# Moving one row tile's load and statistics, and the place of the shift rows, in the start of a fused adaLN block

## The chip, the cores and the metric

The kernel runs on one core of a Trainium2 chip. The metric is device time in microseconds (us) of one launch; the times shown are medians over several launches. A profile belongs to one launch: its "span" reaches from the first instruction of the program to the last, and the launch's own time is a little longer than that.

The engines that matter are TensorE (PE; its weight loads have rows of their own, PEld), VectorE (DVE), ScalarE (ACT), GpSimd (POOL) and the queue of SyncE (SP), from which nearly all transfers are issued. All five work their own instructions in a fixed order and wait for each other by semaphores.

## The reference, cut to what matters

```python
# x: (1, 2048, 1024) bf16, c: (1, 1024); LN has no affine part
sa, ca, ga, sb, cb, gb = (silu(c) @ w_mod).reshape(1, 6, 1, 1024)  # six rows of 1024
h   = layernorm(x) * (1 + ca) + sa
q, k, v = split(h @ wqkv)                      # 32 heads of 32
phi = lambda t: where(t > 0, t + 1, exp(t)) + 1e-6
kv, z = sum_s phi(k) v,  sum_s phi(k)
o   = phi(q) kv / (phi(q) z + 1e-6)
x   = x + ga * (o @ wo)
h   = layernorm(x) * (1 + cb) + sb
out = x + gb * ((silu(h @ w_gate) * (h @ w_up)) @ w_down)
```

Only the first line of h, its "scale" row 1 + ca and its "shift" row sa, and v = h @ wv for the first 512 rows of x are touched by the change.

## The kernel before, in words

The 2048 rows are worked in four chunks of 512, each of four row tiles of 128 rows. A chunk's normalised rows are kept transposed, hT, as eight blocks of 128 features by 512 rows. After the start, the kernel runs K for a chunk, the sums kv, V for the next chunk, Q, the output projection and then the three large FFN products; from about 26 us on this is one nearly unbroken stream of 128x512 matmuls.

The start (lines 466 to 574) is written out by hand, because in the first 26 us the weights are still arriving. Three things set its order.

*The SP queue.* Loads are issued one by one in program order (lines 126 to 154), 256 KB each: row tiles 0, 1 and 2 of x (`load_x`, line 123), the first half of the scale weights `wca[0]` (`load_ca`, line 141; its first quarter goes over ACT's queue), four value-weight blocks `wv` 0 to 3 (`load_block`, line 136), `wca[1]`, row tile 3, `wv` 4 to 7, then `wsa` (the shift's weights, eight blocks) and `wk`. Each load takes one of eight semaphores in turn, so that a load is not issued before the one eight places ahead of it has landed.

*An order by hand on DVE, ACT and POOL.* Everything inside `with in_order(...)` stays in program order on these three engines; PE keeps program order everywhere.

*The trick of the value product.* In the first chunk, v is not computed from h but from hs = layernorm(x) * (1 + ca): the shift's share sa @ wv is one row and is added to the sums later. So v can start as soon as the scale is known for some features. Features 0 to 511 (blocks cc 0 to 3) have their scale as columns in `col0` and `mod_ps` from 32 small matmuls (`ca_cols`); features 512 to 1023 (cc 4 to 7) get it later from `ca_rows` (32 narrow matmuls with `wca[1]`), `mod_turn` (a transpose on DVE), and an addition of one.

For a row tile, DVE takes `bn_stats` over two halves of 512 features and `bn_aggr`, then the variance plus epsilon (`veps`); POOL computes `rstd` = veps to the power -0.5 and `nmr` = -mean * rstd; ACT or DVE writes the normalised tile `xn`. PE turns it (`transpose` into a PSUM tile `tp`), DVE scales the turned blocks from PSUM into `hs` (`scale_first`, `scale_turned`, `scale_to`), and ACT copies `tp` into hT for K and Q.

The value groups are eight pairs (row tile t, half nb of the output columns). The first four, `gs` (t = 0, 1), have accumulators in one PSUM pool; `gs2` (t = 2) and `gs3` (t = 3) follow. `v_mms(hs, gs, accs, lo, hi)` runs the blocks cc from lo to hi for all groups in gs. PE's order before the change is:

- `gs` cc 0; turn the second half of tile 1; `gs` cc 1 and 2; turn all of tile 2 (`tp2`); `gs` cc 3; `ca_rows`;
- `gs2` cc 0 to 3; `gs` cc 4 to 7; `gs2` first group cc 4 to 7; turn tile 3; `gs2` second group cc 4 to 7;
- `gs3` first group; `mod_rows` with `wsa` (the shift rows: 32 narrow matmuls); `gs3` second group; K.

After `mod_rows`, DVE transposes the result (`mod_turn`, line 270), copies it into `sca` (line 568), and then adds the shift and applies the scale to hT in place (`modulate`, line 223, 16 instructions); K's first matmul needs the first of these. The ACT instruction of line 538, silu of `c` as a row, feeds a small POOL transfer (`sc_scratch`, line 581) that a much later step uses.

Row tile 2's statistics are spread over DVE's work for tiles 0 and 1: `bn` is a generator, and its three pieces are taken by `next(bn2)` in lines 486, 491 and 525.

Of the kernel before, what the change touches and what calls it, by code (L numbers as in the profile page):

```python
# [8 lines left out]
ACT = mybir.ActivationFunctionType  # L9
ALU = mybir.AluOpType  # L10
# [11 lines left out]
def kernel(  # L22
# [100 lines left out]
        last_load[0] = eng.dma_start(out=x_sb[:], in_=x2[st * P:(st + 1) * P, :])  # L123
        x_tiles[st] = x_sb

    for st in range(3):
        load_x(st, nc.sync)
    nc.scalar.dma_start(out=c_sb[:], in_=c_v)  # L128

# [5 lines left out]
    def load_block(tiles, view, cc, lo, eng=nc.sync):  # L135
        eng.dma_start(out=tiles[cc // 4][:, cc % 4, :], in_=view[:, cc, lo:lo + D])  # L136

    def load_ca(h, eng0):
        for k in range(4):
            js = slice(2 * k, 2 * k + 2)  # L140
            (eng0 if k == 0 else nc.sync).dma_start(out=wca[h][:, js, :], in_=wm_v[:, js, D + h * NB:D + (h + 1) * NB])  # L141
# [2 lines left out]
    nc.scalar.dma_start(out=sc_row[0:1, :], in_=c)  # L144
    for cc in range(4):
        load_block(wv, wqkv_v, cc, 2 * D)
    load_ca(1, nc.sync)
    load_x(3, nc.sync)
    for cc in range(4, DC):
# [48 lines left out]
    def rstd_of(mv, n):  # L198
        veps = small.tile([P, STC], F32, name="veps")
        last_veps[0] = nc.vector.tensor_scalar_add(out=veps[:, 0:n], in0=mv[:, 0:n, 1], scalar1=LN_EPS)  # L200
        rstd = small.tile([P, STC], F32, name="rstd")
        nc.gpsimd.tensor_tensor(out=rstd[:, 0:n], in0=veps[:, 0:n], in1=neg_half[:].to_broadcast([P, n]), op=ALU.pow)  # L202
        return rstd

    def bn(src, mv_out):
        stats = small.tile([P, NNB, nc.vector.BN_STATS_DIM], F32, name="stats")
        for i in range(NNB):
            nc.vector.bn_stats(out=stats[:, i, :], in_=src[:, i * NB:(i + 1) * NB])  # L208
            yield
        nc.vector.bn_aggr(out=mv_out, in_=stats[:])  # L210
        yield

    def normalise_act(dst, src, mv, rstd, pieces=1):
        nmr = small.tile([P, 1], F32, name="nmr")
        last_nmr[0] = nc.gpsimd.tensor_scalar(out=nmr[:], in0=mv[:, 0, 0:1], scalar1=rstd[:, 0:1], scalar2=-1.0,  # L215
                                op0=ALU.mult, op1=ALU.mult)
        w = src.shape[-1] // pieces
        for i in range(pieces):
            ws = slice(i * w, (i + 1) * w)
            nc.scalar.activation(out=dst[:, ws], in_=src[:, ws], func=ACT.Identity, bias=nmr[:], scale=rstd[:, 0:1])  # L220
# [5 lines left out]
    def turn_tile(xn):  # L226
        tp = acc_b("tp", (DC, P), BF16)
        for cc in range(DC):
            transpose(tp[:, cc, :], xn[:, cc * P:(cc + 1) * P])
        return tp  # L230

    hTs = {}

    def ln1_stats(sc, t):
        x_sb = x_tiles.pop(sc * STC + t)
        mv = small.tile([P, STC, 2], F32, name="mv")
        for _ in bn(x_sb, mv[:, 0, :]):
            pass
        rstd = rstd_of(mv, 1)
        return sc, t, x_sb, mv, rstd  # L240

    def ln1_norm(sc, t, x_sb, mv, rstd, pieces=1):
        xn = k2.tile([P, D], BF16, name="xn", bufs=4)
        normalise_act(xn[:], x_sb[:], mv, rstd, pieces)
        if sc > 0:
            last_load[0] = nc.sync.dma_start_transpose(hTs[sc][:, :, t * P:(t + 1) * P], xn[:])
        return xn
# [229 lines left out]
    with in_order(nc.vector, nc.scalar, nc.gpsimd):  # L477
        mod_ps = acc_b("mod_ps")
        mm(mod_ps[:, 0:DC], lhsT=c_sb[:], rhs=ident[0:DC, 0:DC], start=True, stop=True)
        nc.scalar.activation(out=scT[:], in_=mod_ps[:, 0:DC], func=ACT.Silu)  # L480
        xn0 = ln1_norm(*ln1_stats(0, 0), 2)
        _, _, x1_sb, mv1, rstd1 = ln1_stats(0, 1)
        x2_sb = x_tiles.pop(2)
        mv2 = small.tile([P, STC, 2], F32, name="mv")
        bn2 = bn(x2_sb, mv2[:, 0, :])
        next(bn2)
        xn1 = k2.tile([P, D], BF16, name="xn", bufs=4)
        nc.vector.tensor_scalar(out=xn1[:, 0:NB], in0=x1_sb[:, 0:NB], scalar1=mv1[:, 0, 0:1], scalar2=rstd1[:, 0:1],
                                op0=ALU.subtract, op1=ALU.mult)
        normalise_act(xn1[:, NB:], x1_sb[:, NB:], mv1, rstd1)  # L490
        next(bn2)
        col0 = acc_b("col0")
        cols = [col0[:, 0:1]] + [mod_ps[:, DC + i:DC + i + 1] for i in range(3)]
        tps = [acc_b("tp", (4, H), BF16) for _ in range(2)]

        def turn_half(xn, t, h):
            for i in range(4):
                transpose(tps[h][:, i, t * P:(t + 1) * P], xn[:, (4 * h + i) * P:(4 * h + i + 1) * P])

        def ca_cols(k):  # L500
            for i in range(4):
                for j in (2 * k, 2 * k + 1):
                    mm(cols[i], lhsT=wca[0][:, j, i * P:(i + 1) * P], rhs=scT[:, j:j + 1], start=False,
                       stop=j == DC - 1 and i in (0, 3))

        mm(cols[0], lhsT=ident[:], rhs=base_t[:, 0:1], start=True, stop=False)
        keep_warm(P)
        mm(mod_ps[:, DC:DC + 3], lhsT=ident[:], rhs=base_t[:, 0:3], start=True, stop=False)
        keep_warm(2 * P)
        ca_cols(0)  # L510
        keep_warm(2 * P, P)
        ca_cols(1)
        turn_half(xn0, 0, 0)
        ca_cols(2)
        keep_warm(P)
        turn_half(xn0, 0, 1)
        turn_half(xn1, 1, 0)
        ca_cols(3)
        keep_warm(P)

        def scale_first(cc):
            nc.vector.tensor_scalar(out=hs[:, cc, 0:H], in0=tps[0][:, cc, :], scalar1=cols[cc], scalar2=None, op0=ALU.mult)

        scale_first(0)
        next(bn2)
        rstd2 = rstd_of(mv2, 1)
        for cc in range(1, 4):
            scale_first(cc)
        nc.scalar.copy(out=ca0T[:, 0:1], in_=cols[0])
        nc.scalar.copy(out=ca0T[:, 1:4], in_=mod_ps[:, DC:DC + 3])  # L530
        xn2 = ln1_norm(0, 2, x2_sb, mv2, rstd2)
        nc.scalar.copy(out=hT[:, 0:4, 0:H], in_=tps[0][:])
        nc.vector.tensor_copy(out=sc32[:], in_=scT[:].unsqueeze(2).to_broadcast([P, DC, DH]))
        gs = k_groups[0:4]
        v_mms(hs, gs, accs, 0, 1)
        turn_half(xn1, 1, 1)
        nc.scalar.copy(out=hT[:, 4:8, 0:H], in_=tps[1][:])
        nc.scalar.activation(out=sc_row[0:1, :], in_=sc_row[0:1, :], func=ACT.Silu)
        v_mms(hs, gs, accs, 1, 3)
        tp2 = turn_tile(xn2)  # L540
        for cc in range(4):
            scale_turned(tp2, cc, 2)
        nc.scalar.copy(out=hT[:, :, H:H + P], in_=tp2[:])
        v_mms(hs, gs, accs, 3, 4)
        ca_rows()
        mod_turn(DC + 4, 2 * DC)
        nc.vector.tensor_scalar_add(out=ca0T[:, 4:8], in0=ca0T[:, 4:8], scalar1=1.0)
        for cc in range(4, DC):
            scale_to(hs, hT, cc, 0, H)
        gs2, accs2 = k_groups[4:6], [acc_b("acc") for _ in range(2)]  # L550
        v_mms(hs, gs2, accs2, 0, 4)
        xn3 = ln1_norm(*ln1_stats(0, 3))
        for cc in range(4, DC):
            scale_to(hs, hT, cc, H, H + P)
        v_mms(hs, gs, accs, 4, DC)
        v_evac(0, gs, accs)
        v_mms(hs, gs2[0:1], accs2[0:1], 4, DC)
        tp3 = turn_tile(xn3)
        for cc in range(DC):
            scale_turned(tp3, cc, 3)  # L560
        nc.scalar.copy(out=hT[:, :, H + P:], in_=tp3[:])
        v_mms(hs, gs2[1:2], accs2[1:2], 4, DC)
        v_evac(0, gs2, accs2)
        gs3, accs3 = k_groups[6:8], [acc_a() for _ in range(2)]
        v_mms(hs, gs3[0:1], accs3[0:1])
        mod_rows(lambda j: wsa[j // 4][:, j % 4, :], 0, DC)
        mod_turn(0, DC)
        nc.vector.tensor_copy(out=sca[:], in_=scr[:, :, :, 0])
        v_mms(hs, gs3[1:2], accs3[1:2])
        v_evac(0, gs3, accs3)  # L570
        for lo in (0, H):
            for cc in range(DC):
                modulate(hT, cc, ca1T, saT, lo, lo + H)
        nc.vector.tensor_copy(out=sc32[:], in_=saT.unsqueeze(2).to_broadcast([P, DC, DH]))
# [269 lines left out]
```

## Time and profile before

| | us |
|---|---|
| median of 4 launches | 829.06 |
| lowest and highest | 828.71, 830.18 |
| the profiled launch's own time | 829.04 |
| its span | 827.2 |
| PE busy in the span | 818.6 |
| first value matmul starts | 8.92 |
| shift rows (`mod_rows`) start | 23.28 |
| first K matmul starts | 26.00 |

The page of the profile lists each engine's busy time, the longest chain and the costliest groups; the timeline lists instructions in order of time, equal neighbours merged, with the start, the time covered, engine, line, output and inputs. A matmul of 128x512 is listed with 379 ns, but matmuls overlap: one starts every 0.216 us (64 of them between 40.17 and 54.01). A few matmul records are missing from the trace.

### The profile page before, as it was taken

Reading aid. Unit: us, or ns where it says so; the run is one execution under the profiler, and the core shown is the slowest. Engines: PE = TensorE matmul, PEld = TensorE weight load, DVE = VectorE, ACT = ScalarE, POOL = GpSimd, SP = SyncE. Lnnn points to the kernel's source line nnn. Section 1 sums busy time; section 2 is a strip of 40 time slices with the busy share of each in tenths; the row PEclk is TensorE's granted clock in tenths of the full one; section 3 lists DMA queues with packets and bytes.
Section 4 is the critical chain, followed back from the end, with each engine's and each line's share of the span. In section 5 each row is a group of like instructions: output and inputs, shape, how many; then the busy total and the mean of one; then the engine's idle time right before and its main releaser. Section 6 shows DMA issues by size and latency. Waiting matters only on the chain.

```text
span 827.2 us, 11268 instructions
## 1 busy us (share of the span) xinstructions
PE 818.6 (99%) x4551; PEld 380.5 (46%) x4629; DVE 346.0 (42%) x683; ACT 173.6 (21%) x261; POOL 65.4 (8%) x167
## 2 busy tenths in 40 slices
PE   9999999999999999999999999999999999999998
PEld 6444444444444444444444444444444444444444
DVE  5879778886353344421111353211124432222222
ACT  5545443434111101101111010111111101111000
POOL 3101110120313001000000010000001100000000
PEclk9999999999999999999999999999999999999999
DMA  9988444139995726456252272753405529710011
GB/s 340 308 180 205 115 108 98 44 118 315 374 239 176 258 104 192 140 171 212 81 172 83 69 221 86 253 185 114 141 1 183 148 67 343 238 40 1 19 58 52
DMA packets 143414, 129.33 MB, mean 156 GB/s; under 512 B 58817, under 2 KB 122817, under 8 KB 142850
## 3 DMA queue, kind: packets, MB, share of 16 engines
q1 hardware_dynamic: 139248, 115.36, 46.3%
q0 software_dynamic: 3824, 12.98, 5.0%
q8 instruction: 36, 0.59, 0.3%
q10 hardware_dynamic: 290, 0.27, 0.1%
q14 instruction: 16, 0.13, 0.0%
HBM read 102.24 MB, written 12.72 MB: 139 GB/s over the span
## 4 chain that ended last, share of the span: by engine, by line
PE 95%; DMA 3%; issue 1%; DVE 0%; SPq 0%; ACTq 0%
PE acc L98 87%; PE a_ps L98 7%; DMA wme<-in_w_mod_dram 2%; DMA wk<-in_A_wqkv_dram 1%; DMA x_sb<-in_A_x_dram 1%; PE kvp L98 1%; DVE stats L208 0%; PE den L98 0%; SPq L136 0%; PE wf L98 0%; PE vb L98 0%; ACTq L128 0%; DVE pk L287 0%; SPq L141 0%; DVE e L760 0%
## 5 line engine op out<-in xcount | busy, mean ns | idle before, releaser
L98 PE MATMUL acc<-h2T,wgu 128*128 128x512 bf16 x1756 | 385.7, 379 | 1.9
L98 PEld LDWEIGHTS <-wgu 128*128 128x128 bf16 x1792 | 175.3, 98 | 211.3
L739 DVE TENSOR_TENSOR gu<-acc,e 128x512 bf16<-128x512 f32 x112 | 77.5, 692 | 289.9 <-PE acc L98 278.8
L98 PE MATMUL acc<-wd,gu 128*128 128x512 bf16 (+2 forms) x908 | 195.2, 372 | 0.9
L738 ACT ACTIVATE e<-acc 128x512 f32<-128x512 f32 x112 | 66.9, 597 | 374.8 <-PE acc L98 363.4
L98 PEld LDWEIGHTS <-gu 128*128 128x128 bf16 x924 | 89.3, 98 | 104.4
L760 DVE TENSOR_TENSOR e<-acc,gb_bc 128x512 f32<-128x512 f32 (+2 forms) x33 | 22.3, 675 | 131.6 <-PE acc L98 122.7
L98 PEld LDWEIGHTS <-hT 128*128 128x128 bf16 x448 | 43.6, 98 | 52.5 <-issue 0.4
L98 PE MATMUL a_ps<-wof,pq 128*128 128x512 bf16 x250 | 56.9, 379 | 0.3
L98 PE MATMUL acc<-wk,hT 128*128 128x512 bf16 x249 | 55.7, 379 | 0.8 <-issue 0.5
L98 PE MATMUL acc<-hT,wq 128*128 128x512 bf16 x249 | 55.9, 379 | 0.4 <-issue 0.2
L284 ACT ACTIVATE eb<-acc 128x512 bf16<-128x512 f32 x64 | 37.5, 594 | 60.3 <-PE acc L98 56.6
L220 ACT ACTIVATE xn<-x,nmr,rstd 128x1024 bf16<-128x1024 f32 x16 | 19.8, 1240 | 126.2 <-POOL nmr L215 125.4
L98 PE MATMUL acc<-wv,hT 128*128 128x512 bf16 x189 | 41.8, 379 | 0.2
L707 POOL DMA_DIRECT2D x_scratch<-x x16 | 9.8, 615 | 373.5 <-DVE x L700 373.4
L98 PEld LDWEIGHTS <-pq 128*128 128x128 bf16 x256 | 25.0, 98 | 30.2
L98 PEld LDWEIGHTS <-wq 128*128 128x128 bf16 x256 | 24.6, 98 | 30.7 <-issue 1.7
L285 DVE TENSOR_SCALAR eb<-eb 128x512 bf16<-128x512 bf16 x64 | 18.2, 289 | 26.2 <-ACT eb L284 26.2
L700 DVE TENSOR_TENSOR x<-a_ps,x_sb 128x512 f32<-128x512 f32 x32 | 22.1, 691 | 8.6 <-PE a_ps L98 7.9
L202 POOL TENSOR_TENSOR rstd<-veps,neg_half 128x1 f32<-128x1 f32 x32 | 18.0, 564 | 91.7 <-DVE veps L200 69.7
L220 ACT ACTIVATE xn<-x_sb,nmr,rstd 128x1024 bf16<-128x1024 bf16 (+1 forms) x17 | 19.5, 1163 | 15.9 <-POOL nmr L215 15.8
L763 DVE TENSOR_TENSOR ob<-e,x1r 128x512 bf16<-128x512 f32 (+2 forms) x33 | 22.3, 675 | 1.0
(106 smaller groups left out, 331.6 us busy)
## 6 DMA issues: line engine op xcount, KB each, us to landing
wgu<-in_B_w_gate_dram SPq DMA_DIRECT2D x28, 1024.0 KB, 7.1
wgu<-in_B_w_up_dram SPq DMA_DIRECT2D x28, 1024.0 KB, 8.1
x_sb<-in_A_x_dram SPq DMA_DIRECT2D x32, 256.0 KB, 5.3
x_scratch<-x POOLq DMA_DIRECT2D x16, 512.0 KB, 3.4
x1r<-x_scratch SPq DMA_DIRECT2D x31, 256.0 KB, 2.8
wd<-in_B_w_down_dram SPq DMA_DIRECT2D x7, 1024.0 KB, 5.7
rbc<-rden_scratch POOLq DMA_DIRECT2D x16, 256.0 KB, 6.9
out_dram<-ob SPq DMA_DIRECT2D x31, 128.0 KB, 1.7
```

The lines of the kernel that those rows point to most:

```text
L98: return tc.keep_in_program_order(nc.tensor.matmul(out, lhsT=lhsT, rhs=rhs, start=start, stop=stop))
L202: nc.gpsimd.tensor_tensor(out=rstd[:, 0:n], in0=veps[:, 0:n], in1=neg_half[:].to_broadcast([P, n]), op=ALU.pow)
L220: nc.scalar.activation(out=dst[:, ws], in_=src[:, ws], func=ACT.Identity, bias=nmr[:], scale=rstd[:, 0:1])
L284: nc.scalar.activation(out=e[:], in_=acc, func=ACT.Exp)
L285: nc.vector.tensor_scalar(out=e[:], in0=e[:], scalar1=1.0, scalar2=PHI_EPS, op0=ALU.min, op1=ALU.add)
L700: nc.vector.tensor_tensor(out=x1[:, ns], in0=a_ps[:], in1=x_t[:, ns], op=ALU.add)
L707: nc.gpsimd.dma_start(out=x1_dram[st * P:(st + 1) * P, :], in_=x1[:])
L738: nc.scalar.activation(out=sg[:], in_=ps[0][:], func=ACT.Silu)
L739: gm = nc.vector.tensor_tensor(out=guT[sc][f // GPT][:, f % GPT, :], in0=ps[1][:], in1=sg[:], op=ALU.mult)
L760: nc.vector.tensor_tensor(out=yt, in0=y_ps, in1=gb_bc[:, ns], op=ALU.mult)
L763: nc.vector.tensor_tensor(out=ob, in0=yt, in1=x1r, op=ALU.add)
```

## The change

Row tile 2 of x is loaded after `wv` blocks 0 and 1 and not as the third load of all. Its statistics are no longer spread over the work on tiles 0 and 1: `bn` becomes a plain function, and tile 2's statistics stand after the casts of the first half's scaling. Tile 2 is then normalised as tile 1 is, its first 512 features on DVE and the rest on ACT (`norm_split`). PE turns its first half after `gs` cc 3, and `gs2` cc 0 and 1 follow at once; `ca_rows` comes after that, then the turning of tile 2's second half, and `gs2` cc 2 and 3. The first of tile 0 and 1's scalings is cut into two of 128 columns. The silu on `c` as a row moves behind ACT's copy of tile 2. The shift rows move from between the two groups of `gs3` into the middle of the second.

```diff
-    for st in range(3):
+    for st in range(2):
         load_x(st, nc.sync)
...
     for cc in range(4):
         load_block(wv, wqkv_v, cc, 2 * D)
+        if cc == 1:
+            load_x(2, nc.sync)
...
+    def norm_split(src, mv, rstd):
+        xn = k2.tile([P, D], BF16, name="xn", bufs=4)
+        nc.vector.tensor_scalar(out=xn[:, 0:NB], in0=src[:, 0:NB], scalar1=mv[:, 0, 0:1], scalar2=rstd[:, 0:1],
+                                op0=ALU.subtract, op1=ALU.mult)
+        normalise_act(xn[:, NB:], src[:, NB:], mv, rstd)
+        return xn
...
         _, _, x1_sb, mv1, rstd1 = ln1_stats(0, 1)
-        x2_sb = x_tiles.pop(2)
-        mv2 = small.tile([P, STC, 2], F32, name="mv")
-        bn2 = bn(x2_sb, mv2[:, 0, :])
-        next(bn2)
...
-        next(bn2)
+        xn1 = norm_split(x1_sb, mv1, rstd1)
...
-        scale_first(0)
-        next(bn2)
-        rstd2 = rstd_of(mv2, 1)
+        scale_first(0, 0, P)
+        scale_first(0, P, H)
         for cc in range(1, 4):
-            scale_first(cc)
+            scale_first(cc, 0, H)
...
-        xn2 = ln1_norm(0, 2, x2_sb, mv2, rstd2)
...
         v_mms(hs, gs, accs, 0, 1)
         turn_half(xn1, 1, 1)
         nc.scalar.copy(out=hT[:, 4:8, 0:H], in_=tps[1][:])
-        nc.scalar.activation(out=sc_row[0:1, :], in_=sc_row[0:1, :], func=ACT.Silu)
-        v_mms(hs, gs, accs, 1, 3)
-        tp2 = turn_tile(xn2)
+        _, _, x2_sb, mv2, rstd2 = ln1_stats(0, 2)
+        xn2 = norm_split(x2_sb, mv2, rstd2)
+        v_mms(hs, gs, accs, 1, 4)
+        tp2 = acc_b("tp", (DC, P), BF16)
+        for cc in range(4):
+            transpose(tp2[:, cc, :], xn2[:, cc * P:(cc + 1) * P])
         for cc in range(4):
             scale_turned(tp2, cc, 2)
-        nc.scalar.copy(out=hT[:, :, H:H + P], in_=tp2[:])
-        v_mms(hs, gs, accs, 3, 4)
+        gs2, accs2 = k_groups[4:6], [acc_b("acc") for _ in range(2)]
+        v_mms(hs, gs2, accs2, 0, 2)
         ca_rows()
         mod_turn(DC + 4, 2 * DC)
         nc.vector.tensor_scalar_add(out=ca0T[:, 4:8], in0=ca0T[:, 4:8], scalar1=1.0)
         for cc in range(4, DC):
             scale_to(hs, hT, cc, 0, H)
-        gs2, accs2 = k_groups[4:6], [acc_b("acc") for _ in range(2)]
-        v_mms(hs, gs2, accs2, 0, 4)
+        for cc in range(4, DC):
+            transpose(tp2[:, cc, :], xn2[:, cc * P:(cc + 1) * P])
+        nc.scalar.copy(out=hT[:, :, H:H + P], in_=tp2[:])
+        nc.scalar.activation(out=sc_row[0:1, :], in_=sc_row[0:1, :], func=ACT.Silu)
+        v_mms(hs, gs2, accs2, 2, 4)
...
         v_mms(hs, gs3[0:1], accs3[0:1])
+        v_mms(hs, gs3[1:2], accs3[1:2], 0, 4)
         mod_rows(lambda j: wsa[j // 4][:, j % 4, :], 0, DC)
         mod_turn(0, DC)
         nc.vector.tensor_copy(out=sca[:], in_=scr[:, :, :, 0])
-        v_mms(hs, gs3[1:2], accs3[1:2])
+        v_mms(hs, gs3[1:2], accs3[1:2], 4, DC)
```

More of the change, by code (lines that the diff above doesn't have):

```diff
@@ L208, in bn @@
             nc.vector.bn_stats(out=stats[:, i, :], in_=src[:, i * NB:(i + 1) * NB])
-            yield
         nc.vector.bn_aggr(out=mv_out, in_=stats[:])
-        yield
     def normalise_act(dst, src, mv, rstd, pieces=1):
@@ L236, in ln1_stats @@
         mv = small.tile([P, STC, 2], F32, name="mv")
-        for _ in bn(x_sb, mv[:, 0, :]):
-            pass
+        bn(x_sb, mv[:, 0, :])
         rstd = rstd_of(mv, 1)
@@ L482 @@
         _, _, x1_sb, mv1, rstd1 = ln1_stats(0, 1)
-        x2_sb = x_tiles.pop(2)
-        mv2 = small.tile([P, STC, 2], F32, name="mv")
-        bn2 = bn(x2_sb, mv2[:, 0, :])
-        next(bn2)
[L487 to L490, printed above, removed]
-        next(bn2)
+        xn1 = norm_split(x1_sb, mv1, rstd1)
         col0 = acc_b("col0")
@@ L519, with scale_first @@
         keep_warm(P)
-        def scale_first(cc):
-            nc.vector.tensor_scalar(out=hs[:, cc, 0:H], in0=tps[0][:, cc, :], scalar1=cols[cc], scalar2=None, op0=ALU.mult)
-        scale_first(0)
-        next(bn2)
-        rstd2 = rstd_of(mv2, 1)
+        def scale_first(cc, lo, hi):
+            nc.vector.tensor_scalar(out=hs[:, cc, lo:hi], in0=tps[0][:, cc, lo:hi], scalar1=cols[cc], scalar2=None, op0=ALU.mult)
+        scale_first(0, 0, P)
+        scale_first(0, P, H)
         for cc in range(1, 4):
-            scale_first(cc)
+            scale_first(cc, 0, H)
         nc.scalar.copy(out=ca0T[:, 0:1], in_=cols[0])
         nc.scalar.copy(out=ca0T[:, 1:4], in_=mod_ps[:, DC:DC + 3])
-        xn2 = ln1_norm(0, 2, x2_sb, mv2, rstd2)
         nc.scalar.copy(out=hT[:, 0:4, 0:H], in_=tps[0][:])
```

## The prediction

> **What bounds the kernel.** I read the page first, then the chain in order of time, then the timelines of PE, DVE, POOL and PEld up to 45 us. The page says that nothing but PE counts:
>
> ```profile
> span 827.2 us, 11268 instructions
> PE 818.6 (99%) x4551; PEld 380.5 (46%) x4629; DVE 346.0 (42%) x683; ACT 173.6 (21%) x261; POOL 65.4 (8%) x167
> ```
>
> The profiled launch took 829.04 us, 1.8 us more than its span and equal to the median of 829.06; the sum goes against 829.04. After 26 us the change touches nothing, and PE's work is the same in kind and number (the built order has as many PE instructions as before), so the time can move only by PE's idle time before some 45 us. PE's order there:
>
> ```profile
> 8.92 1.04 PE L98 MATMUL acc<-wv,hs 128*128 128x512 bf16 x3
> ...
> 11.74 0.61 PE L101 MATMUL tp<-ident,xn 128*128 128x128 bf16 x8
> 12.19 1.03 PE L98 MATMUL acc<-wv,hs 128*128 128x512 bf16 x4
> 13.14 0.78 PE L98 MATMUL mod_ps<-wme,sc 128*32 128x128 bf16 x32
> 13.85 6.46 PE L98 MATMUL acc<-wv,hs 128*128 128x512 bf16 x27
> 20.15 0.61 PE L101 MATMUL tp<-ident,xn 128*128 128x128 bf16 x8
> 20.59 2.75 PE L98 MATMUL acc<-wv,hs 128*128 128x512 bf16 x12
> 23.28 1.06 PE L98 MATMUL mod_ps<-wme,sc 128*32 128x256 bf16 x32
> 24.27 1.90 PE L98 MATMUL acc<-wv,hs 128*128 128x512 bf16 x7
> ```
>
> From start to start: a 512-wide matmul costs 0.216, four turnings 0.22 (half of 12.19 - 11.74), `ca_rows` 0.71 (13.85 - 13.14), `mod_rows` 0.99 (24.27 - 23.28). Idle time hides in such rows; the weight loads show it, where 0.12 between two loads is the normal pace and the rest is a stall:
>
> ```profile
> 17.56 0.53 PEld L98 LDWEIGHTS <-hs 128*128 128x128 bf16 x3 [0.36 <-issue]
> ...
> 33.15 0.31 PEld L98 LDWEIGHTS <-hT 128*128 128x128 bf16 x2 [0.36 <-issue]
> ```
>
> So 0.24 at 17.56 (`wv` 6 lands about 17.5, as the next user of its semaphore is issued then) and 0.24 at 33.15 (an accumulator that DVE frees at 33.11). Starts within `ca_rows` show 0.13 more, waiting for the last `wca[1]` load (about 13.6), and Q's first matmul at 40.17 0.12. All of PE's idle time after 8.92 is thus 0.73 us: the change has little to win and more to lose. The other engines' rows that the sums use:
>
> ```profile
> 6.69 0.69 DVE L208 BATCH_NORM_STATS2 stats<-x_sb 128x6 f32<-128x512 bf16 x1
> 7.44 0.41 DVE L488 TENSOR_SCALAR xn<-x_sb,mv,rstd 128x512 bf16<-128x512 bf16 x1
> ...
> 12.46 0.86 DVE L277 TENSOR_SCALAR hs<-tp,e 128x128 bf16<-128x128 bf16 x4 [2.28 <-PE tp L101]
> 13.96 0.32 DVE L270 STREAM_TRANSPOSE e<-mod_ps 128x128 f32<-128x128 f32 x1 [0.65 <-PE mod_ps L98]
> ...
> 25.08 4.19 DVE L223 TENSOR_SCALAR hT<-hT,sca 128x256 bf16<-128x256 bf16 x16
> ```
>
> ```profile
> 14.64 0.74 POOL L581 DMA_DIRECT2D sc_scratch<-sc_row  x1 [4.33 <-ACT sc_row L538]
> 17.19 0.59 POOL L202 TENSOR_TENSOR rstd<-veps,neg_half 128x1 f32<-128x1 f32 x1 [1.81 <-DVE veps L200]
> ```
>
> **The change, step by step.**
>
> *Loads.* Loads land one after another, 0.67 apart (5.11, 5.84, 6.50, 7.19 ...), with the DMA engines at a share of 1.03 or more from 4 us to 26. Tile 2 moves from the slot 5.84 to that of 9.22. Three `wca[0]` loads and `wv` 0 and 1, which it is moved behind, come one slot earlier, issued 0.44 earlier on SP; everything behind keeps its slot, and `wv` 2 and 3 their issue, since the place of `wv` 1, now tile 2's, waits for the landing at 5.11 as before. ACT's and POOL's queues have no load moved past. A slot could be worth 0.67, but PE was not waiting there: `ca_cols` followed the warming matmuls without a gap, and the first scaling (8.50) needs tile 0's second half from ACT (7.72), tile 1's first half from DVE (7.86) and 12 small PE steps. Taken 0; bounds -0.67 and 0.
>
> *DVE up to 8.9.* Two `bn_stats` (0.69), `bn_aggr` (0.20) and `veps` (0.15) leave. They filled waits: line 488 at 7.44 waited for POOL's `rstd`, line 522 at 8.50 for the last column from PE at 8.45. Gone cover costs nothing, as DVE then idles. The halved first scaling lasts 0.28 (line 277's mean) for 0.36: -0.08, of which PE, in its last warming matmul until about 8.86, can use 0.06. **First value matmul 8.86: -0.06.**
>
> *Tile 2's values.* DVE: 8.50, two halves 0.40, three scalings 0.79, the copy of line 533 0.20; so `bn_stats` at 9.9 (the tile landed at 9.22). Tile 1's own chain gives the rest: 1.71 from the first `bn_stats` (5.06) to the end of `veps` (6.77), 1.09 from there to the end of line 488 (7.86). So the first half of xn is there at 12.70 and can be turned from 12.76. PE: 8.86 + 16 x 0.216 + 0.22 = 12.53. **Wait 0.23** (0.05 if DVE keeps the shortest spacing of its rows; 0.5 if each DVE step is as late as the slowest).
>
> *Turning to matmul with nothing between.* Before, `gs` cc 3 and `ca_rows` stood between tile 2's turning and its first product. Now it follows at once: the last of four turnings starts at 12.92; 0.33 from there to DVE (12.13 to 12.46), 0.28 for the scaling, 0.05 to PE: 13.58. PE is free at 12.98. **Wait 0.60** (0.43 if the scaling need not wait for all four; 0.7).
>
> *Old stalls.* PE is now late enough for `ca_rows` (14.53) not to wait for its weights, nor cc 6 (about 17.9) for `wv` 6: **-0.13 and -0.24**. `ca_rows`' last start moves from 13.70 to 14.97; 1.18 later (13.70 to 14.88) the first of `scale_to` is done, and PE meanwhile turns four and runs four: 0.15 + 0.22 + 0.86, just enough. Taken 0. Tile 2's copy in hT is done by 16.6, its later scaling by 19.3, its use starts at 19.7: covered.
>
> *Tile 3.* `bn_stats` behind `scale_to` moves with `ca_rows` by 1.27: its `veps` ends at 18.36, not 17.09. The silu of line 538 now follows ACT's copy of tile 2 (from 15.6), ends at 17.6 and releases POOL's transfer, 17.8 to 18.6 (whose reader, line 407, comes at 62 us); tile 3's `rstd`, behind it on POOL's queue, starts at 18.6, xn at 19.55, done 20.8 (18.18 to 19.42 before). PE gets there at 20.5. **Wait 0.34** (0 to 0.5). Queued behind it on ACT are four casts of `v`, the first done at 21.4; their accumulators are wanted at 22.1, which covers it.
>
> *Shift rows.* From `mod_rows`' end to the first `modulate` done took 24.27 to 25.42: 1.15, covered by eight matmuls (1.73). Four are left: 0.86. The last shift block lands at 23.6, well before either place, so nothing is gained. **Wait 0.34** (0.28 to 0.45), 1.15 + 0.05 - 0.86.
>
> K then starts at 26.0 - 0.06 + 0.23 + 0.60 - 0.37 + 0.34 + 0.34 = 27.1.
>
> *K.* The 16 `modulate` end 1.5 later. The next chunk's `bn_stats` started at 29.62 when its load landed; they now start at about 31.0, 1.35 late, and DVE's first freed accumulator 1.15 late (the built order takes 0.18 of small work out from before it), against a PE 1.08 late: the stall of 0.24 becomes 0.3 to 0.4. **+0.1** (0 to 0.5). Q's 0.12 goes, as the fifth accumulator is now freed earlier relative to PE: **-0.12** (0).
>
> Sum: 1.08 + 0.1 - 0.12 = +1.06. With the shortest spacings in place of tile 1's measured chain it is about 0.75. I take **+0.9: 829.9 us**. Low ends together: -0.67 + 0.05 + 0.43 - 0.37 + 0 + 0.28 + 0 - 0.12 = -0.4, 828.6. High ends: 0 + 0.5 + 0.7 - 0.37 + 0.5 + 0.45 + 0.5 = +2.3, 831.3.
>
> [...] The window view grants PE a clock of 1.00 from 4 us on, through the old stalls of 0.24 and 0.13; at the start a 128x256 warming pass takes 0.43 (until about 5.7 us), later 0.21. [...]
>
> **Rivals.**
>
> *Early slots pass through (no loss).* If the head really follows the `wca[0]` loads and the new waits take their low ends: 828.6. For it: loads are on the chain up to 29.6. Against: the 0.04-wide joints between warming matmuls and `ca_cols`.
>
> *Slower by over 0.2%: DVE and ACT bound K.* DVE is busy 6.99 of the 7.15 us from 26.00 to 33.15. If its 1.35 is not absorbed, or the built order's two normalisations in a row on ACT (2 x 1.24 ahead of K's fifth exponential) hold back an accumulator, 1.2 to 2.3 come on top: 831.1 to 832.2. It decides once an accumulator is freed over 0.8 later than in the sum. Against: PE's own delay gives DVE as much time back.
>
> *Slower: the clock falls.* If waits of 0.83 within a microsecond close the gate, PE pays half speed until it opens again; the first opening came after about 4.8 us of PE work (0.91 to 5.7, by the steps of the warming passes), so some 2.4 us more: 832.3. Against: the 1.00 above.
>
> *Faster by over 0.2%.* It needs 1.66 us, but all old stalls (0.73) and a whole load slot (0.67) make 1.40: 827.6 at best, which takes something no row shows.
>
> **How the numbers follow.** A measurement of this kernel can tell about 0.2% (1.66 us) from no change. Likeliest case, 829.2 to 830.7: 0.70. Early slots: 0.10. DVE and ACT: 0.11. Clock: 0.05. Faster: 0.04. Within 0.2% are the first two less 0.04 of the likeliest one's upper tail: 0.76; slower 0.20; faster 0.04. The range goes from 828.6 to 831.3, the ends of the bounds; it leaves out the clock, the faster case and half of the DVE case.
>
> **What would show it.** In the profile after: first value matmul at about 8.86; tile 2's turnings at 12.7 and their product at 13.6, DVE's line for `scale_turned` named as releaser; POOL's `sc_scratch` transfer at 17.8 right ahead of `rstd`; tile 3's turnings at 20.85 waiting for ACT; K's first matmul at 27.1 waiting for `modulate`; a stall near 34.3; from 45 us on the same steps as before. It is wrong if K starts before 26.5, if matmuls after 13 us step by more than 0.22, or if stalls appear after 45 us.

## The result, and the profile after

The changed kernel took 830.22 us (median of 39 launches, 830.06 to 833.34) against 829.28 for the kernel before (59 launches, 828.71 to 831.78). The ratio is 1.0013, 95% interval 1.0009 to 1.0018, so the change costs 1.1 us (0.75 to 1.5). The profiled launch's span is 828.4, 1.2 more than before. The page of the kernel after:

```profile
span 828.4 us, 11268 instructions
PE 818.1 (99%) x4551; PEld 379.7 (46%) x4629; DVE 346.5 (42%) x685; ACT 173.6 (21%) x261; POOL 65.4 (8%) x167
```

PE has the same 4551 instructions and no more busy time; the span grew around them. The timeline of PE after (start, time covered, engine, line, operation, output and inputs, count, and in brackets idle time and what ended it):

```profile
7.18 0.40 PE L101 MATMUL tp<-ident,xn 128*128 128x128 bf16 x4 [0.70 <-ACT xn L220]
...
8.96 1.04 PE L98 MATMUL acc<-wv,hs 128*128 128x512 bf16 x3
...
12.85 0.40 PE L101 MATMUL tp<-ident,xn 128*128 128x128 bf16 x4
13.70 1.04 PE L98 MATMUL acc<-wv,hs 128*128 128x512 bf16 x4 [0.45 <-ACT xn L220]
14.67 0.63 PE L98 MATMUL mod_ps<-wme,sc 128*32 128x128 bf16 x32
15.23 0.40 PE L101 MATMUL tp<-ident,xn 128*128 128x128 bf16 x4
15.68 5.13 PE L98 MATMUL acc<-wv,hs 128*128 128x512 bf16 x23
20.96 0.62 PE L101 MATMUL tp<-ident,xn 128*128 128x128 bf16 x8 [0.15 <-ACT xn L220]
...
24.97 1.06 PE L98 MATMUL mod_ps<-wme,sc 128*32 128x256 bf16 x32
...
27.18 7.08 PE L98 MATMUL acc<-wk,hT 128*128 128x512 bf16 x32 [0.18 <-DVE hT L223]
34.46 7.07 PE L98 MATMUL acc<-wk,hT 128*128 128x512 bf16 x31 [0.20 <-DVE pk L293]
41.37 13.98 PE L98 MATMUL acc<-hT,wq 128*128 128x512 bf16 x63
55.18 1.89 PE L98 MATMUL acc<-wk,hT 128*128 128x512 bf16 x8
```

The bracket counts from the modelled end of the last matmul, so it is smaller than the wait. The waits below are start to start, less the normal step (0.216 behind a 512-wide matmul, 0.056 behind a turning). Four waits are new: 0.21 ahead of tile 2's turning (12.85), 0.61 between it and its product (13.70; the bracket names ScalarE, but PE waits for VectorE there, as the experiment "Work put behind the turning" shows), 0.32 ahead of tile 3's turning (20.96) and 0.35 at K's start (27.18). The stall in K grew from 0.24 to 0.37 (34.46). The 0.13 inside `ca_rows`, the 0.24 at `wv` 6 and the 0.12 ahead of Q are gone. Together: 0.21 + 0.61 + 0.32 + 0.35 + 0.13 - 0.13 - 0.24 - 0.12 = 1.13. The next step of the program, K of the second chunk, starts at 55.18 against 54.01: the 1.13, and the 0.04 by which the first value matmul was later in this launch. The span's 1.2 is this shift.

The launches of one kernel spread over 1 to 3 us here; three of the profiled ones show PE reaching its full rate late in the first microseconds (last section). A ratio from five rounds is good to about 0.0009, or 0.75 us. So each experiment is also read in its trace, over a stretch behind those first microseconds: from the first value matmul to the first matmul of the sums kv (8.92 to 55.83 before, 8.96 to 57.00 after). It is 46.91 us before and 48.04 after, 1.13 more.

### The profile page after: what moved, and what is told of

Its sections match the earlier page's. It is cut to its first block, busy times and chain, and to the rows that moved or that the text cites. A ratio compares the mean times of both kernels' runs of the same rounds, so it can differ in the third digit from the quotient of the medians.

```text
span 828.4 us, 11268 instructions
## 1 busy us (share of the span) xinstructions
PE 818.1 (99%) x4551; PEld 379.7 (46%) x4629; DVE 346.5 (42%) x685; ACT 173.6 (21%) x261; POOL 65.4 (8%) x167
## 4 chain that ended last, share of the span: by engine, by line
PE 96%; DVE 2%; issue 1%; ACT 0%; DMA 0%; POOL 0%; DVEq 0%
PE acc L98 88%; PE a_ps L98 7%; DVE stats L210 1%; PE kvp L98 1%; DVE hT L223 1%; ACT xn L220 0%; DMA x_sb<-in_A_x_dram 0%; PE den L98 0%; PE mod_ps L98 0%; POOL rstd L204 0%; PE tp L101 0%; DVE hs L520 0%; PE wf L98 0%; DVE hs L279 0%; POOL nmr L215 0%
## 5 line engine op out<-in xcount | busy, mean ns | idle before, releaser
L704 DVE BATCH_NORM_STATS2 stats<-x 128x6 f32<-128x512 f32 x32 | 22.1, 693 | 1.0
```

The costliest lines, as they stand in the source:

```text
L704: nc.vector.bn_stats(out=stats[:, nb, :], in_=x1[:, ns])
```

## The experiments

**One part alone: the shift rows.**

```diff
--- kernel before
         v_mms(hs, gs3[0:1], accs3[0:1])
+        v_mms(hs, gs3[1:2], accs3[1:2], 0, 4)
         mod_rows(lambda j: wsa[j // 4][:, j % 4, :], 0, DC)
...
-        v_mms(hs, gs3[1:2], accs3[1:2])
+        v_mms(hs, gs3[1:2], accs3[1:2], 4, DC)
```

> The kernel before, with one edit: the shift rows in the middle of the last value group. If the new waits add up as predicted: the wait behind the shift rows (0.35 in the profile after) appears here by itself, K's first matmul about 0.35 to 0.45 later against the landing of row tile 0, the time +0.3 to +0.5 us (ratio 1.0004 to 1.0006). Rival, the shift-row move carries the whole loss: about +1 us (1.0012). Rival, K's own stall absorbs it: no difference (1.0000).

Measured: 829.93, ratio 1.0007 (0.9999 to 1.0016). PE in the timeline:

```profile
27.11 7.08 PE L98 MATMUL acc<-wk,hT 128*128 128x512 bf16 x32 [0.18 <-DVE hT L223]
34.40 7.07 PE L98 MATMUL acc<-wk,hT 128*128 128x512 bf16 x31 [0.21 <-DVE pk L287]
```

The wait at K's start (0.34) is here by itself, and so is the grown stall in K (0.37): K's part of the loss hangs on the shift rows. In this launch a late load put the first value matmul at 9.85, which by itself took away the old stall at `wv` 6; so the stretch is 46.91 + 0.34 + 0.13 - 0.12 - 0.24, and 0.07 for a longer load wait inside `ca_rows`: 47.09. The move is a part of the loss, not the whole; that is read in the trace, since the interval of the ratio takes in the rival's 1.0012 too.

**The same part undone.**

```diff
--- changed kernel
-        v_mms(hs, gs3[1:2], accs3[1:2], 0, 4)
         mod_rows(lambda j: wsa[j // 4][:, j % 4, :], 0, DC)
...
-        v_mms(hs, gs3[1:2], accs3[1:2], 4, DC)
+        v_mms(hs, gs3[1:2], accs3[1:2])
```

> The changed kernel, with the shift rows back between the two groups of the last row tile. If the waits add up: K's first matmul about 0.35 to 0.4 earlier than in the changed kernel, its stall near 34.4 us smaller, and the time 0.4 to 0.7 us below the changed kernel's, that is +0.3 to +0.6 against before. Rival, the shift-row move carries the whole loss: equal to before. Rival, VectorE bounds K whatever PE does: equal to the changed kernel, +1.

Measured: 830.01, ratio 1.0013 (1.0005 to 1.0021): by medians 0.2 under the changed kernel, too little for this measurement. The profiled launch had PE at half rate up to 14 us, so its stretch can't be used; from tile 2's first product (16.85) to the sums kv (59.54) it takes 42.69, and the changed kernel 43.30. The 0.61 that it saves is 0.35 at K's start and the whole stall in K, less 0.10 that comes back ahead of Q. The trace agrees with the expectation; the times alone don't decide.

**The load's place undone.** The changed kernel with tile 2 as third load.

```diff
-    for st in range(2):
+    for st in range(3):
         load_x(st, nc.sync)
...
-        if cc == 1:
-            load_x(2, nc.sync)
```

> The changed kernel, with row tile 2 loaded as the third load again; the order of all engines stays the changed one. If the waits lie in the engines' order: tile 2's statistics still start when VectorE is through with the first half's scaling (10.0 us), the same waits of 0.21, 0.61 and 0.32, time equal to the changed kernel's within 0.2 us, +1 against before. Rival, the later load is the cause: statistics at or before 9.3, the wait ahead of tile 2's turning gone, time 0.3 or more below the changed kernel's.

Measured: 830.56, ratio 1.0020 (1.0011 to 1.0029), by medians 0.3 above the changed kernel's where 0.2 was allowed; the stretch is 48.04, that of the changed kernel to the hundredth. VectorE and PE:

```profile
11.38 0.28 DVE L527 COPY sc<-scT 128x256 bf16<-128x256 bf16 x1
11.58 1.28 DVE L208 BATCH_NORM_STATS2 stats<-x_sb 128x6 f32<-128x512 bf16 x2
```

```profile
14.43 0.40 PE L101 MATMUL tp<-ident,xn 128*128 128x128 bf16 x4
15.28 1.04 PE L98 MATMUL acc<-wv,hs 128*128 128x512 bf16 x4 [0.45 <-ACT xn L218]
```

(This launch reached its first value matmul 1.58 later than the changed kernel's.) The tile had landed at 6.09, and its statistics still follow the copy without a gap: they wait for their turn on VectorE, not for the load. The later load is not the cause.

**The load's place alone.** The kernel before with only the load moved; the order on the engines stays.

```diff
-    for st in range(3):
+    for st in range(2):
         load_x(st, nc.sync)
...
+        if cc == 1:
+            load_x(2, nc.sync)
```

> The kernel before, with one edit: row tile 2 loaded behind the first two value-weight blocks, every engine's order as before. VectorE's first statistics piece of tile 2 stands ahead of tile 1's normalisation there, so it waits for the load (9.2 to 9.7 us, in place of a start at 6.69): if only the gathered statistics make the late load free, tile 1 is normalised about 2.9 later, the first value matmul starts at 11.5 to 11.9 (8.92 before), the two old stalls of 0.37 go, and the time is 2.0 to 2.6 above before (ratio 1.0024 to 1.0031). Rival, the load's place costs nothing in any order: first value matmul within 0.2 of 8.92, time equal to before.

Measured: 832.60, ratio 1.0038 (1.0027 to 1.0049), more than expected; the profiled launch, at 830.92, was among the shortest of ten (830.77 to 834.01).

```profile
9.49 0.69 DVE L210 BATCH_NORM_STATS2 stats<-x_sb 128x6 f32<-128x512 bf16 x1 [2.46 <-DMA x_sb<-in_A_x_dram]
```

```profile
10.56 0.40 PE L101 MATMUL tp<-ident,xn 128*128 128x128 bf16 x4 [2.10 <-DVE xn L490]
...
11.45 1.04 PE L98 MATMUL acc<-wv,hs 128*128 128x512 bf16 x4
```

In the old order VectorE sits on this load with tile 1's normalisation behind it, and the first value matmul comes 2.5 later (expected 2.6 to 3.0). The stretch is 0.64 shorter, since all old stalls but a part of Q's are covered by the delay. So the gathered statistics are what makes the late load free. Why other launches lose up to 3 us more than the profiled one was not seen.

**Work put behind the turning.** The changed kernel with `ca_rows` ahead of tile 2's first product.

```diff
             scale_turned(tp2, cc, 2)
+        ca_rows()
         gs2, accs2 = k_groups[4:6], [acc_b("acc") for _ in range(2)]
         v_mms(hs, gs2, accs2, 0, 2)
-        ca_rows()
```

> The changed kernel, with the second scale half's narrow matmuls put between the turning of tile 2's first half and its first product. If the 0.61 there is the scaling's latency with no PE work to cover it: that wait goes; in its place the narrow matmuls wait 0.1 to 0.35 for their last weights (landed about 13.6); tile 3's wait of 0.32 shrinks, since its statistics start earlier; time 0.3 to 0.5 below the changed kernel's, +0.5 to +0.7 against before. Rival, the first product waits for something other than the scaling: wait stays at 0.6, and the time at +1.

Measured: 829.81, ratio 1.0005 (0.9997 to 1.0014); the stretch is 47.33, 0.71 under the changed kernel's.

```profile
12.84 0.40 PE L101 MATMUL tp<-ident,xn 128*128 128x128 bf16 x4
13.16 0.88 PE L98 MATMUL mod_ps<-wme,sc 128*32 128x128 bf16 x32
13.97 1.04 PE L98 MATMUL acc<-wv,hs 128*128 128x512 bf16 x3
...
20.25 0.61 PE L101 MATMUL tp<-ident,xn 128*128 128x128 bf16 x8
```

The 0.61 is gone; `ca_rows` now waits 0.25 inside itself for its last weights (its rows cover 0.88 and not 0.63); tile 3's wait is gone as well, as its statistics hang on `ca_rows` and GpSimd's transfer now comes behind its `rstd`. 0.61 + 0.32 - 0.25 = 0.68 of the 0.71.

One rival for the 0.61 is left: in the profile after, the bracket at 13.70 names ScalarE's half of `xn`, which ran from 12.88 to 13.69. The kernel with the shift rows undone settles it:

```profile
14.54 0.81 ACT L220 ACTIVATE xn<-x_sb,nmr,rstd 128x512 bf16<-128x512 bf16 x1 [0.34 <-POOL nmr L215]
...
16.01 0.39 PE L101 MATMUL tp<-ident,xn 128*128 128x128 bf16 x4
...
16.85 1.04 PE L98 MATMUL acc<-wv,hs 128*128 128x512 bf16 x4 [0.45 <-DVE hs L283]
```

There ScalarE was through 1.5 us before the product; the wait is 0.61 all the same, and the bracket names VectorE. So the largest term is the latency of one turning and one scaling with no PE work in front of it.

**GpSimd's queue ahead of tile 3.** The changed kernel with one silu moved back.

```diff
         nc.scalar.copy(out=hT[:, 4:8, 0:H], in_=tps[1][:])
+        nc.scalar.activation(out=sc_row[0:1, :], in_=sc_row[0:1, :], func=ACT.Silu)
...
         nc.scalar.copy(out=hT[:, :, H:H + P], in_=tp2[:])
-        nc.scalar.activation(out=sc_row[0:1, :], in_=sc_row[0:1, :], func=ACT.Silu)
```

> The changed kernel, with ScalarE's silu of c as a row back in its early place, so that GpSimd's small transfer is through before tile 3's statistics. If that transfer holds tile 3's rstd: the transfer starts at about 15 us, rstd follows veps at 18.4 and not 18.7, and PE's wait ahead of tile 3's turning falls from 0.32 to about 0.1 us or less; the time 0.2 to 0.3 below the changed kernel's 830.2. Rival, ScalarE or VectorE hold tile 3, not GpSimd: the wait stays within 0.05 of 0.32.

Measured in one launch: 830.12. GpSimd's timeline of the kernel after, and then of this one with PE's row:

```profile
17.93 0.74 POOL L584 DMA_DIRECT2D sc_scratch<-sc_row  x1 [5.09 <-ACT sc_row L552]
18.71 0.56 POOL L204 TENSOR_TENSOR rstd<-veps,neg_half 128x1 f32<-128x1 f32 x1
```

```profile
13.21 0.74 POOL L584 DMA_DIRECT2D sc_scratch<-sc_row  x1 [0.35 <-ACT sc_row L534]
18.58 0.59 POOL L204 TENSOR_TENSOR rstd<-veps,neg_half 128x1 f32<-128x1 f32 x1 [4.63 <-DVE veps L202]
...
20.87 0.62 PE L101 MATMUL tp<-ident,xn 128*128 128x128 bf16 x8
```

The transfer did hold `rstd`, but only for 0.13: `veps` is not ready before 18.49. PE's wait falls from 0.32 to 0.21 (0.1 or less was expected), and the stretch by 0.11. Both stories are true in part: a third of this wait is the transfer, two thirds are tile 3's statistics, which come later because `ca_rows` does.

**All waits but one covered.** The changed kernel with three of the edits above together.

```diff
+        nc.scalar.activation(out=sc_row[0:1, :], in_=sc_row[0:1, :], func=ACT.Silu)
...
+        ca_rows()
         gs2, accs2 = k_groups[4:6], [acc_b("acc") for _ in range(2)]
         v_mms(hs, gs2, accs2, 0, 2)
-        ca_rows()
...
-        nc.scalar.activation(out=sc_row[0:1, :], in_=sc_row[0:1, :], func=ACT.Silu)
...
-        v_mms(hs, gs3[1:2], accs3[1:2], 0, 4)
...
-        v_mms(hs, gs3[1:2], accs3[1:2], 4, DC)
+        v_mms(hs, gs3[1:2], accs3[1:2])
```

> The changed kernel with three of its moves undone: the narrow matmuls between tile 2's turning and its product, the silu early, the shift rows between the last two groups; the later load of tile 2, its statistics in one piece and its split normalisation stay. If the loss is the sum of the waits: K's first matmul about 1.2 earlier than in the changed kernel, at 26.0 within 0.2, and the time equal to before within 0.3 us (ratio 0.9996 to 1.0004). Rival, the later load or the gathered statistics carry part of the loss: +0.5 or more against before.

Measured: 829.74, ratio 1.0000 (0.9991 to 1.0009).

```profile
12.85 0.40 PE L101 MATMUL tp<-ident,xn 128*128 128x128 bf16 x4
13.18 0.52 PE L98 MATMUL mod_ps<-wme,sc 128*32 128x128 bf16 x24
13.90 0.29 PE L98 MATMUL mod_ps<-wme,sc 128*32 128x128 bf16 x8 [0.20 <-DMA wme<-in_w_mod_dram]
...
26.26 14.15 PE L98 MATMUL acc<-wk,hT 128*128 128x512 bf16 x64
```

The stretch is 47.28: of the 1.13, 0.76 went, and 0.37 stays. Of that, 0.22 lies ahead of K (17.30 from the first value matmul to K, 17.08 before): the 0.21 at tile 2's turning, which is the price of the gathered statistics, and a longer load wait inside `ca_rows`, less the old 0.24 at `wv` 6. The other 0.15 is in K and Q, where a new step of 0.46 at 45.79 waits for VectorE to free an accumulator; why it is late there is open. K starts at 26.26, a little outside the 0.2 expected. By the stretch, the three moves carry two thirds of the loss; the ratio cannot tell the 0.37 that stays from nothing.

**The stall in K.** The changed kernel, and then the kernel before, with one edit outside the change: the next chunk's second tile gets its statistics after VectorE has freed K's first accumulator.

```diff
         if sc + 1 < NSC:
-            ln1(sc + 1, [last_on[nc.vector.engine]] * 2 + [i.ins for i in last_phi[2:4]] if sc == 0 else [last_phi[-5].ins] * STC)
+            ln1(sc + 1, [last_on[nc.vector.engine]] + [i.ins for i in last_phi[1:4]] if sc == 0 else [last_phi[-5].ins] * STC)
```

> The changed kernel, with one edit behind the changed part: the statistics of the next chunk's second tile come after VectorE has freed K's first accumulator, not before. If the stall near 34.4 is VectorE freeing that accumulator late behind four statistics passes (2.5 us): the stall of 0.37 goes, and the time is 0.2 to 0.4 below the changed kernel's. Rival, ScalarE's exponential or a load holds it: the stall stays, time equal to the changed kernel's; or it comes back 0.2 or more at a later accumulator.

> The kernel before, with one edit: the statistics of the next chunk's second tile after VectorE has freed K's first accumulator. If that late accumulator makes the stall of 0.24 at 33.15: it goes, Q's 0.12 at 40.17 may go with it, and the time is 0.2 to 0.4 below before (ratio 0.9995 to 0.9998). Rival, the four statistics passes then hold a later accumulator: a stall of 0.2 or more behind 34 us, time equal to before.

Measured: on the changed kernel 830.01, ratio 1.0010 (1.0001 to 1.0019) to the kernel before, and a stretch of 47.68, 0.36 less; on the kernel before 828.88, ratio 0.9990 (0.9982 to 0.9999), and a stretch of 46.55, 0.36 less. The kernel before, without the edit and then with it:

```profile
26.00 14.21 PE L98 MATMUL acc<-wk,hT 128*128 128x512 bf16 x63
40.17 14.00 PE L98 MATMUL acc<-hT,wq 128*128 128x512 bf16 x63
```

```profile
26.17 13.98 PE L98 MATMUL acc<-wk,hT 128*128 128x512 bf16 x63
39.99 13.98 PE L98 MATMUL acc<-hT,wq 128*128 128x512 bf16 x63
```

K's matmuls cover 13.98 and not 14.21, and Q starts 13.82 behind K's start and not 14.17: the stall of 0.24 and Q's 0.12 are gone. So the stall was VectorE, with four statistics passes in front of the accumulator. By medians this version is 0.4 us under the kernel before, with an interval that just leaves out 1, and 1.3 under the changed one.

**Two attempts at a start with no waits.** The first starts from the changed kernel. Tile 2 is loaded behind `wca[0]`, its statistics stand around the first scalings, tile 3 is normalised on both engines, and the edit on K is in; PE's order becomes:

```diff
--- changed kernel
-        v_mms(hs, gs, accs, 1, 4)
+        v_mms(hs, gs, accs, 1, 3)
...
             scale_turned(tp2, cc, 2)
+        v_mms(hs, gs, accs, 3, 4)
         gs2, accs2 = k_groups[4:6], [acc_b("acc") for _ in range(2)]
         v_mms(hs, gs2, accs2, 0, 2)
...
-        v_mms(hs, gs, accs, 4, DC)
+        v_mms(hs, gs, accs, 4, 6)
+        v_mms(hs, gs2, accs2, 4, 6)
+        v_mms(hs, gs, accs, 6, DC)
...
-        tp3 = turn_tile(xn3)
+        tp3 = acc_b("tp", (DC, P), BF16)
+        for cc in range(4):
+            transpose(tp3[:, cc, :], xn3[:, cc * P:(cc + 1) * P])
...
+        v_mms(hs, gs2[0:1], accs2[0:1], 6, DC)
+        for cc in range(4, DC):
+            transpose(tp3[:, cc, :], xn3[:, cc * P:(cc + 1) * P])
...
-        v_mms(hs, gs3[1:2], accs3[1:2], 0, 4)
```

> A version meant to have no exposed wait on PE in the start: tile 2 loaded behind the first scale weights, its first statistics before the first scaling and the rest behind the second, its first half turned behind block 2 and its product behind block 3, the narrow matmuls after two blocks of tile 2, blocks 4 and 5 of tile 2 ahead of blocks 6 and 7 of tiles 0 and 1, tile 3 normalised and turned in halves, the shift rows between the last two groups, and the next chunk's second statistics behind K's first freed accumulator. If the launch time is PE's idle time before 45 us, as the sum had it: K's first matmul at 25.5 to 25.8 (26.0 before), no stall above 0.1 in K, and the time 0.4 to 0.8 us below before (ratio 0.9990 to 0.9995). Rival, loads bound the start once PE is ahead: a wait for a value-weight or shift block of 0.2 to 0.4 in place of those removed, time equal to before within 0.2.

Measured: 830.76, ratio 1.0018 (1.0009 to 1.0028), and a stretch of 48.10; a miss.

```profile
13.59 0.38 PE L98 MATMUL acc<-wv,hs 128*128 128x512 bf16 x1 [0.41 <-ACT hT L540]
14.51 0.81 PE L98 MATMUL acc<-wv,hs 128*128 128x512 bf16 x3 [0.54 <-ACT hT L544]
...
22.57 0.38 PE L101 MATMUL tp<-ident,xn 128*128 128x128 bf16 x4 [0.52 <-DVE hs L285]
```

Neither theory holds. Tile 2's accumulators come from the same four PSUM buffers as the turned halves of tiles 0 and 1 (`acc_b`), and ACT, which now normalises tile 2 first, copies those halves out late (0.57 and 0.70 lost). Tile 3's second turning waits for VectorE's scaling of the first (0.68); that it is so because both halves lie in one PSUM tile is argued, not shown. The stalls of K and Q are gone here too, and don't make up for it.

The second starts from the kernel before, with its loads and its early statistics. Tiles 2 and 3 are normalised on both engines, tile 3's statistics are spread between the scalings, the edit on K is in, and PE's order becomes:

```diff
--- kernel before
-        tp2 = turn_tile(xn2)
+        tp2 = acc_b("tp", (DC, P), BF16)
+        for cc in range(4):
+            transpose(tp2[:, cc, :], xn2[:, cc * P:(cc + 1) * P])
...
         v_mms(hs, gs, accs, 3, 4)
+        gs2, accs2 = k_groups[4:6], [acc_b("acc") for _ in range(2)]
+        v_mms(hs, gs2, accs2, 0, 2)
         ca_rows()
...
+        for cc in range(4, DC):
+            transpose(tp2[:, cc, :], xn2[:, cc * P:(cc + 1) * P])
...
-        v_mms(hs, gs2, accs2, 0, 4)
+        v_mms(hs, gs2, accs2, 2, 4)
...
-        v_mms(hs, gs, accs, 4, DC)
+        v_mms(hs, gs, accs, 4, 6)
+        v_mms(hs, gs2[0:1], accs2[0:1], 4, 6)
+        v_mms(hs, gs, accs, 6, DC)
```

> The kernel before, loads in its order, with other work in front of each of its old stalls: tile 2's first half turned ahead of block 3 and its first two products behind it, so that the narrow matmuls come after their weights; its second half turned behind them; two blocks of tile 2 between blocks 5 and 6 of tiles 0 and 1; tiles 2 and 3 normalised on both engines; and the statistics edit on K. If launch time is PE's idle time in the start: 0.13, 0.24, 0.24 and 0.12 go, K's first matmul at 25.6 (26.0 before), and the time 0.5 to 0.7 below before (ratio 0.9991 to 0.9994). Rival, a PSUM buffer freed late by ScalarE, or tile 3's statistics, sets a new wait of 0.2 to 0.9 ahead of 21 us: time equal to before or above.

Measured: 829.05, ratio 0.9992 (0.9983 to 1.0001); no better than the edit on K alone.

```profile
13.85 0.63 PE L98 MATMUL mod_ps<-wme,sc 128*32 128x128 bf16 x32
...
14.86 1.68 PE L98 MATMUL acc<-wv,hs 128*128 128x512 bf16 x7
17.17 3.61 PE L98 MATMUL acc<-wv,hs 128*128 128x512 bf16 x16 [0.63 <-DMA wv<-in_A_wqkv_dram]
```

`ca_rows` has no wait and no stall is left at K, but PE now runs into `wv` 5, which landed at 17.13 in this launch (15.47 in the profile before): 0.79. The stretch is 46.94. The wait has the size that the rival named, but neither of its two makers: once PE was ahead in this launch, a load took the gain. How often that block is late was not measured; the shortest launch took 828.44.

**A long wait and the clock.** The changed kernel with unused work on VectorE.

```diff
+        for _ in range(10):
+            extra = small.tile([P, nc.vector.BN_STATS_DIM], F32, name="extra")
+            nc.vector.bn_stats(out=extra[:], in_=x2_sb[:, 0:NB])
         for cc in range(4):
             scale_turned(tp2, cc, 2)
```

> The changed kernel, with ten more statistics passes of 512 columns on VectorE, their results unused, ahead of the scaling of tile 2's first half. They take about 6.1 us there, so that PE waits some 6 us between tile 2's turning and its product, in place of 0.61. If a long wait halves PE's clock: matmuls behind it step by 0.43 in place of 0.216, for 3 us or more, and the time is 8 us or more above the changed kernel's. Rival, PE keeps its rate through a wait of 6 us: steps of 0.216 at once, time 5.0 to 5.8 above the changed kernel's. The clock falling in the changed kernel itself would need the first, and at a wait ten times shorter.

Measured in one launch: 838.68. PE's timeline, and the windows (stretch, its length, busy time of PE, PEld, DVE, ACT and POOL, then the granted clock, the DMA share and GB/s):

```profile
14.52 0.40 PE L101 MATMUL tp<-ident,xn 128*128 128x128 bf16 x4
20.65 1.89 PE L98 MATMUL acc<-wv,hs 128*128 128x512 bf16 x4 [5.73 <-DVE hs L283]
```

```profile
16.00:17.00 1.00, 0.00 (x0) 0.00 (x0) 1.00 (x3) 0.00 (x0) 0.00 (x0) 1.00 1.07 412
17.00:17.50 0.50, 0.00 (x0) 0.00 (x0) 0.50 (x2) 0.00 (x0) 0.00 (x0) 0.67 1.05 406
17.50:18.00 0.50, 0.00 (x0) 0.00 (x0) 0.50 (x2) 0.00 (x0) 0.00 (x0) 0.50 1.14 422
...
23.50:24.00 0.50, 0.50 (x6) 0.49 (x6) 0.41 (x2) 0.00 (x0) 0.00 (x0) 0.51 1.06 389
24.00:24.50 0.50, 0.41 (x3) 0.20 (x2) 0.39 (x3) 0.42 (x1) 0.00 (x0) 1.00 1.06 389
```

A wait of 5.9 us does halve the clock, from 17.2 to 24.0. Four products cover 1.89 and not 1.04, and from 20.65 to K's start PE needs 15.02, not 13.48: 1.54 lost to the clock, beside 5.28 for the longer wait. The other 1.67 of the 8.46 is a late opening of the clock before the first value matmul in this launch, so the 8 that I named is met by accident. In the changed kernel itself the products behind the 0.61 step by 0.216 at once; the rival of a falling clock is out.

## Why the prediction was right

I forecast 829.9 within 828.6 to 831.3, with no change over 0.2% as the likeliest; it became 830.22, a loss of 0.13%. The steps, as the prediction named them:

| step | forecast | profile after | runs |
|---|---|---|---|
| first value matmul | 8.86 | 8.96, with tile 0 landed 0.11 later | |
| *Loads* | 0 | 0 | undone, the stretch is unchanged; alone, +2.5 at the first value matmul |
| *Tile 2's values*, wait | 0.23 | 0.21 | stays with all else covered |
| *Turning to matmul with nothing between* | 0.60 | 0.61 | gone with `ca_rows` in between |
| *Old stalls* | -0.13, -0.24 | both gone | |
| *Tile 3*, wait | 0.34 | 0.32 | 0.11 of it the transfer |
| *Shift rows*, wait | 0.34 | 0.35 | 0.34 alone |
| *K* | +0.1 | +0.13 | comes and goes with the shift rows |
| Q | -0.12 | -0.12 | |

The sum worked out was +1.06 and the stretch shows +1.13. I then took +0.9, on the way to the 0.75 for engines that keep the shortest spacings of their rows. They did not: VectorE began the statistics at 10.00 and xn's first half was there at 12.79, as tile 1's chain of 1.71 and 1.09 had it (forecast 9.9 and 12.70). Where the same chain of instructions has been measured once in the trace, its own length is the better number; the 0.16 taken off was a loss of accuracy, too small for the launch times to show (the medians are 0.94 apart). Of the 0.3 between 829.9 and 830.22, 0.24 is the base: the forecast went out from 829.04, and the 59 launches of the kernel before have a median of 829.28.

Three things were looser than these sizes show. In *Tile 3* the sum runs through GpSimd's transfer and does not say what it adds: `rstd` starts 0.10 behind `veps` without it (17.09 and 17.19 before), so by the forecast's own numbers it adds 0.14 (18.60 for 18.46), and the later statistics cost 0.2 by themselves. The runs show the same: 0.13 at `rstd`, 0.11 at PE, and 0.21 without it. One of the signs did not come as said: at tile 2's product the bracket names ScalarE and not VectorE's scaling, for the reason given above. And not every load kept its slot: tile 2 was said to land at 9.22 and landed at 9.70, and those behind it came about 0.5 late too (tile 3's 14.74, 14.25 before). VectorE began on tile 2 at 10.00, so 0.3 was left; that no wait hung on it was partly luck.

Of the rivals, early slots passing through fell in the profile after: the first load of `wca[0]` on SP landed at 5.78 and not 6.50, but PE then waited 0.70 for tile 0 from ScalarE (the row at 7.18), the first value matmul came at 8.96, and the new waits did not take their low ends; VectorE and ScalarE as bounds of K were there only as the 0.13; the clock did not fall in the changed kernel, whose longest new wait is 0.61; it fell in a wait of 5.9.

## What to carry to other kernels

When PE is 99% busy, judge a reordering by the work that stands between each producer and its consumer: from the last turning's start over a scaling from PSUM to the product took 0.67 us here, a little more than three 512-wide matmuls, and a move that takes such work away from in between costs the difference. Price it by the length of the same chain elsewhere in the trace. What a stall is worth taking out is settled by what PE meets next: the edit that removed K's stall kept its 0.36 us, since the matmuls behind it waited for nothing, while what two attempts took out at 12 to 18 us went to a late load in one and to PSUM buffers in the other.

## What the runs showed of the hardware

PE's full rate opens at very different moments, with the same work on PE from 0.91 us on: by the steps of the matmuls between 4.2 and 6.2 us in five of the 14 profiled launches and before 8.6 in six more, but at 9.9 with the load put back (eight turnings from 9.13 cover 0.98, and 0.61 in the kernel before), at about 10.3 with the long wait (two 128x128 passes cover 0.78 from 8.57 and 0.51 from 10.25), and at 14 with the shift rows undone. So the 4.8 us of PE work that the prediction counted ahead of the opening is no fixed amount. In the launch with the shift rows undone the matmuls step by 0.43 up to 14 us, while the granted clock in the window view reads 1.00 (first PE's timeline, then the windows):

```profile
12.95 3.22 PE L98 MATMUL acc<-wv,hs 128*128 128x512 bf16 x12
```

```profile
12.00:14.00 2.00, 2.00 (x9) 1.02 (x8) 1.31 (x4) 1.52 (x2) 0.54 (x1) 1.00 1.10 361
```

The twelve matmuls cover 2.75 in the changed kernel's trace. The column reads 1.00 wherever the trace holds no clock record: this trace and that of the shift rows alone hold none at all, and the first records of the kernels before and after begin when the steps change (5.72 and 4.21). So the column can't be trusted at the start of a launch, and the 1.00 that the prediction took from it for 4 to 5.7 us says nothing; steps from start to start tell the rate. This launch took 832.74, 3.2 above the shortest of its kernel; the one with the load put back took 831.77, 1.6 above its shortest. Nothing in the change touches this.

With the long wait the column does show the fall: 0.67 for 17.00 to 17.50, 0.50 behind it, 1.00 again from 24.00. The clock stayed low for 6.8 us; it fell 2.3 us after PE's last turning ended (14.92), within an idle time of 5.73. In the kernel with the load moved alone PE was idle for 2.10 ahead of its turnings at 10.56, and these came at full rate (four cover 0.40). So in these two launches an idle time of 2.10 left the clock as it was and one of 5.73 did not. How long an idle time has to be, and what sets the moment of a fall or an opening, was not measured.
